# A two-segment hand-over in an attention plus gated feed-forward block: where the attention's buffers are closed, where a norm takes its rows from, and when weights and pieces are made

## The chip, the cores and the metric

One core of a Trainium2 chip runs the kernel. The metric is the device time of one execution in microseconds (us). The kernel before took 910.24 us (median of 3 runs, 908.57 to 913.8). All engines are named as in the profile: PE (TensorE matmul), PEld (its weight loads), DVE (VectorE), ACT (ScalarE), POOL (GpSimd), SP (SyncE, which issues nearly all DMAs).

## What is computed

The reference is a transformer block on x of 2048 x 512 in float32, with a modulation vector for each half:

```python
mod = (silu(c) @ w_mod).reshape(..., 6, 1, -1)          # sa, ca, ga, sb, cb, gb
h = layernorm(x) * (1 + ca) + sa
x = x + ga * attention(h)                               # "A"
h = layernorm(x) * (1 + cb) + sb
x = x + gb * ((h @ w_gate) * (h @ w_up)) @ w_down       # "B"
```

The attention has 32 heads of 16 and works in 4 segments of 512 rows. Within a segment it is a causal softmax, and its result is mixed with what a memory (M, z), summed over the earlier segments, answers to the queries. The output projection is `wo`. The second half is a bilinear feed-forward with 1376 hidden columns and no nonlinearity.

## The kernel before

**Number form.** Matmuls in float32 quality are made of three in a rounded format: each operand is split into a high part (an ACT copy that rounds) and a low part (a subtraction), and high x high, low x high and high x low are added up in PSUM. So every operand that PE reads costs one ACT copy and one subtraction on DVE or POOL. The weight halves are called cwH and cwL, those of the feed-forward's input bH and bL, those of the hidden values mH and mL, those of w_down dH and dL.

**Attention, lines 241 to 390 and 1061 to 1109.** The loop over `v` takes units of four heads (32 units, eight to a segment), each in five slots. A slot has matmuls of queries with keys for the row maximum (`q_step`, reduced on DVE), matmuls for the exponentials (`k_step`: one two-bank PSUM tile `lk`, one ACT `Exp` into `pt`, one or two triangular selects on POOL), and in slot 1 the product with the values (`av_step`, tile `tb`), then its transposition and division (`t_step`, tile `tr`, output `orow`). Other work is filled in between by the generators `fill_a` and `fill_b`: projections of the next segment, the memory, and, for finished segments, the output projection: `wo_op` transposes the attention's rows and splits them (op, oH, oL), `wo_mm` multiplies by `wo` (wops), `wo_add` (line 489) adds the result to the input rows `xr` and stores the sum to DRAM (`x1d`).

**Second norm, `lnC`, line 501.** It loads the four row tiles of a segment from `x1d`, takes mean and variance (DVE `cst`, `cmv`), the reciprocal root (ACT `csd` and `cy`, then five small POOL operations on `cya`, `cyb` and `cy`), normalises in place on DVE, transposes on PE (`ctp`, in the order 2, 3, 0, 1) and scales on ACT into `chf`. In the kernel before, segment 0 runs inside `fill_b`, segment 1 behind the attention's loop (line 1119) with tiles loaded back from `x1d`, segments 2 and 3 during the feed-forward (line 1387).

**Feed-forward, lines 1134 to 1417.** The 2048 rows are done as two halves `p` of two segments each. Each product with w_gate and w_up is a block product by Winograd's seven-multiplication scheme: `build(p)` makes seven pieces of the input out of `chf` (four differences `t` on POOL for two halves each, eight in all, then bH on ACT and bL on DVE), and `wprep` makes seven blocks out of two column tiles of weights: one load `cr` (512 KB), four small sums and differences `cs` on POOL, three ACT copies cwH and three POOL subtractions cwL. A `unit` (line 1284) is seven groups of six matmuls (line 1186) into PSUM tiles Z, Y and X, with ACT copies p5, p1, y and DVE additions c0, c1, c2 between them. Gate and up units alternate; POOL or DVE multiplies the two and `split` makes mH and mL. `wdprep` loads and scales w_down (`crd`) and makes dH and dL. `down` is six matmuls into a PSUM tile `acc` (line 1242) and a DVE addition to the row tile `xa` (line 1245). `prepare(n + 2)` runs in steps during unit n.

**Buffers.** Tiles come from pools with a number of buffers for each tag: `ap` (attention), `pw` (weights of the attention, then oH and oL), `wp` (wo raw, rows for wo_op), `bc` and `pb` (opened when the projections of the last segment are done), and `pc`, opened only when `ap`, `pw`, `wp` and `pb` are closed (lines 1128 to 1134), which holds all tiles of the feed-forward but chf and one of three weight sets.

**Order.** PE's order is written out by hand: every matmul depends on the one before it (`pe`, line 72), and DMAs and some DVE work are pinned to a place in it (`pin`). On the other engines a scheduler orders the instructions when the program is built, and each engine and the DMA queue of SP then run theirs strictly in that order. In the kernel before, the first weight set is prepared inside `fill_b` during the projection of segments 1 and 2; the pieces of the first half and the second weight set come behind the last `wo_add` (lines 1378 to 1381).

Of the kernel before, what the change touches and what calls it, by code (L numbers as in the profile page):

```python
# [57 lines left out]
def tile_kernel(ctx, tc, x, wq, wk_, wv, wo, beta, w_gate, w_up, w_down, c, w_mod, out):  # L58
# [306 lines left out]
    def t_step(u):  # L365

        s, g, jq = u // 8, u // 2 % 4, u % 2
        ug = u // 2
        h0 = jq * HQ
        if jq == 0:  # L370
            orows[ug] = ap.tile([P, 4, HG, DH], F32, tag="orow", name=f"orow{ug}", bufs=2)
# [29 lines left out]
    def wprep(n, tag, pool, rpool):  # L401

        nm, i = units[n % NU]
        raw = rpool.tile([P, KT, 2, P], F32, tag=f"raw{n % 2}", name=f"cr{n}", bufs=1)
        wh = pool.tile([P, 7, 2, P], F32R, tag=f"wh{tag}", name=f"cwH{n}", bufs=1)
        wl = pool.tile([P, 7, 2, P], F32R, tag=f"wl{tag}", name=f"cwL{n}", bufs=1)
        wslot[n] = wh, wl
        views = [w.rearrange("(k p) f -> p k f", p=P)[:, :, i * P:] for w in (w_gate, w_up)]
        gp = nc.gpsimd
        if nm == "x":  # L410
            m = ft[LAST][1]
            for j in range(2):
# [6 lines left out]
        pin(nc.sync.dma_start(raw.rearrange("p k r c -> p k (r c)"), views["gu".index(nm)][:, :, 0:2 * P]))  # L419
# [9 lines left out]
        gp.tensor_sub(S[:, 2], A(0, 0), A(1, 0))  # L429
        gp.tensor_sub(S[:, 3], A(0, 1), S[:, 1])  # L430
        yield
        top = raw[:, :, 0].rearrange("p (c k) f -> p c k f", c=2)
        for d, v in ((slice(4, 6), top), (6, A(1, 1)), (slice(0, 4), S)):
            act.activation(wh[:, d], v, AF.Copy)  # L434
            gp.tensor_sub(wl[:, d], v, wh[:, d].bitcast(F32))  # L435
            yield
# [34 lines left out]
    def xr_load(s, pool, tag="xr"):  # L471
        xrs = []
        for t in range(4):
            xr = pool.tile([P, D], F32, tag=tag, name=f"xr{s}_{t}", bufs=4)
            pin(nc.sync.dma_start(xr, x[rows(s, t), :]))
            xrs.append(xr)
        return xrs
# [20 lines left out]

    hfs = {}

    def lnC(s, pool, hpool, xpool, tag, nb, bk):

        xt = []
        for t in range(4):
            a = xpool.tile([P, D], F32, tag=tag, name=f"x1_{s}_{t}", bufs=nb)
            pin(nc.sync.dma_start(a, x1d[s][t]))
            xt.append(a)
        yield 0.1
# [376 lines left out]

    def open_b():
        close(papool)
        B["bcpool"], B["bc"] = open_pool(name="bc", bufs=1, side="right", reuse_waits="tile")
        B["pbpool"], B["pb"] = open_pool(name="pb", bufs=2, reuse_waits="tile")

    def wo_ops(s, rw, us):
# [77 lines left out]
    def fill_b():  # L969
# [3 lines left out]
            yield None  # L973
        us2 = []
        op2 = wo_op(2, B["o", 2], us2)
        xr1 = xr_load(1, pb)
        small = lambda name: bank(name, small=True)
# [134 lines left out]
    nq = [0]  # L1112

    def lqbank(name):
        nq[0] ^= 1
        return pst((P, 512), f"lq{nq[0]}", name)

    pb = B["pb"]
# [3 lines left out]
    btag[:] = ["sm"]  # L1122
    run(wo_op(3, o3, us3, (NG - 1,), True))
    run(lg)
    for t in range(4):
        run(wo_row(ps3[t], t, us3, (NG - 1,)))
        wo_add(3, t, xr3[t], ps3[t])
    close(B["pbpool"])
    close(pwpool)
    close(apool)  # L1130
    close(wppool)
    vec.eng = nc.vector

    pcpool, pc = open_pool(name="pc", bufs=2, reuse_waits="tile")
    bc = B["bc"]
    NT, NM = 13, 12

    def tmp(name):
        return pc.tile([P, L], F32, tag="t", name=name, bufs=NT)

    pieces = {}

    def build(p):

        def emit(j, srcs):
            hi = pc.tile([P, 2, L], F32R, tag=f"bh{j}", name=f"bH{p}_{j}", bufs=1)
            lo = pc.tile([P, 2, L], F32R, tag=f"bl{j}", name=f"bL{p}_{j}", bufs=1)
            for k in range(2):
                act.activation(hi[:, k], srcs[k], AF.Copy)
                vec.tensor_sub(lo[:, k], srcs[k], hi[:, k].bitcast(F32))  # L1150
# [54 lines left out]

    def split(p, f, c, h):
        n = ft[f][1]
        mH = pc.tile([P, L], F32R, tag="m", name=f"mH{p}_{f}_{c}", bufs=NM)
        mL = pc.tile([P, L], F32R, tag="m", name=f"mL{p}_{f}_{c}", bufs=NM)
        act.activation(mH[0:n], h[0:n], AF.Copy)  # L1210
        vec.tensor_sub(mL[0:n], h[0:n], mH[0:n].bitcast(F32))  # L1211
        mids[p, f, c] = mH, mL

    def wdprep(p, f):
        f0, n = ft[f]
        r = tmp(f"crd{p}_{f}")
        hi = pc.tile([P, D], F32R, tag="wdh", name=f"dH{p}_{f}", bufs=4)
        lo = pc.tile([P, D], F32R, tag="wdl", name=f"dL{p}_{f}", bufs=4)
# [6 lines left out]
        yield  # L1225

    def xtile(p, c, t):
        x1a[p, c, t] = pc.tile([P, D], F32, tag=f"xa{c}{t}", name=f"xa{p}_{c}_{t}", bufs=1)

    def xload2(p, c, t):  # L1230
        pin(nc.sync.dma_start(x1a[p, c, t], x1d[2 * p + c][t]))
# [27 lines left out]
    def finish(p, nm, f, c, v, psum):  # L1259

        n = ft[f][1]
        if nm == "g":
            if psum:
                r = tmp(f"gs{p}_{f}_{c}")
                act.activation(r[0:n], v[0:n], AF.Copy)
                v = r
            gs[p, f, c] = v
# [2 lines left out]
        (vec if psum else nc.gpsimd).tensor_mul(g[0:n], g[0:n], v[0:n])  # L1270
        split(p, f, c, g)

    def add(name, a, b, n=P):
        r = tmp(name)
        vec.tensor_add(r[0:n], a[0:n], b[0:n])  # L1275
        return r

# [85 lines left out]
    def prepare(n):  # L1363

        if n >= 2 * NU:
            return
        yield from wprep(n, n % 3, bc if n % 3 == 0 else pc, bc if n % 2 == 0 else pc)
        nm, i = units[n % NU]
        if nm == "u":
            yield from wdprep(n // NU, i)  # L1370
# [2 lines left out]
            yield from wdprep(n // NU, LAST)  # L1373

    half = [(c, t) for c in (1, 0) for t in range(4)]
    for c, t in half:
        xtile(0, c, t)
    pr1 = prepare(1)
    for _ in range(6):
        next(pr1)  # L1380
    run(build(0))
    DS = {"g": (1, 5, 6), "u": (1, 2, 4, 5, 6), "x": (1, 4, 6)}
    lgs = []

    def lns():
        for s in (2, 3):
            yield from lnC(s, pc, bc, pc, "t", NT, dbank)

    lg = lns()
    nb = None  # L1390
    for n in range(2 * NU):
        nm, i = units[n % NU]
        pr = prepare(n + 2)
# [5 lines left out]
        for st in (unit if nm != "x" else last_unit)(n):  # L1399
# [13 lines left out]
    d()  # L1413
    tail[1]()
    d(99)
    close(pcpool)
    close(B["bcpool"])


_INS = ["x", "wq", "wk", "wv", "wo", "beta", "w_gate", "w_up", "w_down", "c", "w_mod"]  # L1420
# [23 lines left out]
```

## Time and profile before

| | |
|---|---|
| median of 3 runs | 910.24 us |
| the profiled execution | 910.22 us, span of its instructions 908.5 us |
| instructions | 14393 |
| PE, DVE, POOL, ACT busy | 94%, 72%, 55%, 53% of the span |
| DMA | 105.70 MB, mean 116 GB/s |

Times in the profile count from the span's start. A row of the timeline has the start, the time from its first start to its last end, engine, line, operation, output<-inputs, and in brackets the idle time in front and what ended it. A row of the chain of work that ended last has start, time and what ran. A row of a table of windows has, for each engine, the busy time and the number of instructions, then the clock granted to TensorE as a share of full speed. Matmuls overlap in the pipeline, so one of 0.39 us stands for about 0.23 us of PE's time.

### The profile page before, as it was taken

What the parts mean: (1) busy time and instruction counts of PE and PEld (TensorE: products, weight loads), DVE (VectorE), ACT (ScalarE), POOL (GpSimd) and SP (SyncE); (2) the same over time, 40 slices, a digit from 0 to 9 for tenths busy, and PEclk for the clock granted to TensorE, in tenths of its full rate; (3) what the DMA queues carried; (4) which work ended last, traced back from release to release, by engine and by line L of the source; (5) the groups of instructions that cost most, each with busy time, mean ns of one, the idle gap of its engine ahead of it and who ended that gap; (6) DMA issues with size and microseconds to landing.
All of it is one profiled execution on the core that took longest, in us unless ns stands there. A gap on an engine that the chain in (4) does not pass through costs nothing.

```text
span 908.5 us, 14393 instructions
## 1 busy us (share of the span) xinstructions
PE 853.1 (94%) x4963; PEld 598.7 (66%) x4964; DVE 652.7 (72%) x1712; ACT 479.8 (53%) x732; POOL 502.7 (55%) x615
## 2 busy tenths in 40 slices
PE   8989999999999899999999876999999899999998
PEld 5756655556656565665656554778787777877776
DVE  8698777888788877888885463675849965646644
ACT  3658766787576865776445363343345534233320
POOL 4546535566464763955253169765658995566310
PEclk9999999999999999999999988999999999999999
DMA  7555435454454463564743352312221145111002
GB/s 232 154 149 152 125 99 158 128 158 128 117 158 117 135 169 100 146 194 163 227 153 125 125 209 69 87 56 70 70 61 33 46 127 170 56 46 37 12 1 92
DMA packets 77561, 105.70 MB, mean 116 GB/s; under 512 B 11760, under 2 KB 48624, under 8 KB 77488
## 3 DMA queue, kind: packets, MB, share of 16 engines
q1 hardware_dynamic: 77344, 104.76, 39.0%
q8 instruction: 39, 0.64, 0.3%
q14 instruction: 34, 0.28, 0.1%
q10 hardware_dynamic: 144, 0.02, 0.0%
HBM read 76.43 MB, written 28.05 MB: 115 GB/s over the span
## 4 chain that ended last, share of the span: by engine, by line
PE 68%; DVE 15%; ACT 7%; POOL 3%; DMA 3%; issue 3%; SPq 0%; DVEq 0%; ACTq 0%; POOLq 0%
PE acc L1242 11%; PE tb L85 7%; PE q L85 6%; PE k L85 6%; PE Xg L1186 5%; PE Xu L1186 5%; PE vps L85 5%; DVE q L39 4%; PE wops L85 4%; PE kps L85 3%; PE Yu L1186 3%; PE qps L85 3%; PE Yg L1186 2%; ACT pt L331 2%; PE Zu L1186 1%
## 5 line engine op out<-in xcount | busy, mean ns | idle before, releaser
L39 DVE CUSTOM_DVE_ANT_0 q<-q,cmask 128x384 f32<-128x384 f32 (+3 forms) x512 | 246.5, 508 | 49.5 <-PE q L85 39.3
L331 ACT ACTIVATE pt<-k 128x1024 f32<-128x1024 f32 x160 | 163.8, 1024 | 64.0 <-PE k L85 63.3
L337 POOL TENSOR_SCALAR_AFFINE_SELECT pt<-pt 128x256 f32<-128x256 f32 (+1 forms) x224 | 96.7, 446 | 172.0 <-ACT pt L331 169.6
L85 PE MATMUL q<-kst,qst 96*128 96x384 bf16 (+3 forms) x512 | 101.7, 300 | 10.9 <-DVE nm L39 9.8
L85 PE MATMUL k<-qst,kst 98*128 98x384 bf16 (+3 forms) x512 | 97.6, 303 | 7.1 <-ACT pt L331 7.0
L1245 DVE TENSOR_TENSOR xa<-xa,acc 128x512 f32<-128x512 f32 x95 | 64.8, 682 | 47.4 <-PE acc L1242 45.7
L85 PE MATMUL tb<-pt,v 128*32 128x512 f32 (+3 forms) x1024 | 75.5, 436 | 0.0
L85 PEld LDWEIGHTS <-kst 98*128 98x128 bf16 x512 | 38.0, 99 | 52.0 <-issue 45.8
L39 DVE DVE_READ_ACCUMULATOR2_ANT nm<- 128x1 f32 x512 | 72.0, 141 | 0.0
L1242 PE MATMUL acc<-dH,mL 128*128 128x512 f32 (+1 forms) x174 | 68.5, 394 | 1.3 <-DVE mL L1211 1.3
L1242 PE MATMUL acc<-dH,mH 128*128 128x512 f32 (+1 forms) x174 | 68.5, 394 | 0.0
L1242 PE MATMUL acc<-dL,mH 128*128 128x512 f32 (+1 forms) x174 | 68.2, 392 | 0.0
L85 PEld LDWEIGHTS <-qst 96*128 96x128 bf16 x512 | 43.2, 97 | 37.1 <-issue 13.3
L435 POOL TENSOR_TENSOR cwL<-cs,cwH 128x1024 fp32r<-128x1024 f32 x20 | 52.4, 2624 | 4.0 <-ACT cwH L434 4.0
L85 PEld LDWEIGHTS tb<-pt,v 128*32 128x32 f32 x1024 | 28.7, 109 | 38.6 <-issue 34.6
L435 POOL TENSOR_TENSOR cwL<-cr,cwH 128x512 fp32r<-128x512 f32 (+1 forms) x40 | 43.7, 1112 | 12.7 <-ACT cwH L434 12.7
L1270 POOL TENSOR_TENSOR c0g<-c0g,c0u 128x512 f32<-128x512 f32 x10 | 12.9, 1293 | 60.7 <-DVE c0u L1275 46.6
L1186 PE MATMUL Xu<-bH,cwH 128*128 128x512 f32 (+1 forms) x88 | 36.1, 410 | 6.2 <-DVE c2u L1275 4.0
L363 ACT ACTIVATE tsb<-tb 128x512 f32<-128x512 f32 x32 | 19.0, 594 | 40.2 <-PE tb L85 40.2
L1242 PEld LDWEIGHTS acc<-dH,mL 128*128 128x128 f32 (+1 forms) x174 | 32.8, 189 | 9.3 <-DVE mL L1211 2.3
L1242 PEld LDWEIGHTS acc<-dH,mH 128*128 128x128 f32 (+1 forms) x174 | 32.8, 189 | 8.2 <-ACT mH L1210 0.4
L1242 PEld LDWEIGHTS acc<-dL,mH 128*128 128x128 f32 (+1 forms) x174 | 32.7, 188 | 7.1
(278 smaller groups left out, 2177.4 us busy)
## 6 DMA issues: line engine op xcount, KB each, us to landing
wm<-in_w_mod_dram SPq DMA_DIRECT2D x24, 256.0 KB, 4.1
kd<-k SPq DMA_DIRECT2D x16, 384.0 KB, 2.5
kst<-kd SPq DMA_DIRECT2D x32, 192.0 KB, 3.2
qd<-q SPq DMA_DIRECT2D x16, 384.0 KB, 2.9
qst<-qd SPq DMA_DIRECT2D x32, 192.0 KB, 3.6
cr<-in_w_gate_dram SPq DMA_DIRECT2D x10, 512.0 KB, 4.1
cr<-in_w_up_dram SPq DMA_DIRECT2D x10, 512.0 KB, 3.9
crd<-in_w_down_dram SPq DMA_DIRECT2D x20, 256.0 KB, 2.7
```

The lines of the kernel that those rows point to most:

```text
L39: i = getattr(self.eng, name)(*a, **k)
L85: return pe(nc.tensor.matmul(*a, **k))
L331: ex = act.activation(pt, kp, AF.Exp, scale=0.25)
L337: sels[u, i] = nc.gpsimd.affine_select(w, w, pattern=[[0, w.shape[1]], [1, P]], compare_op=ALU.is_ge, fill=0.0, base=0, channel_multiplier=-1)
L363: act.activation(tsbs[u], tbs.pop(u), AF.Copy)
L435: gp.tensor_sub(wl[:, d], v, wh[:, d].bitcast(F32))
L1186: pe(nc.tensor.matmul(ps[0:n], a, b[:, k], start=first and c == 0, stop=last and c == 5, skip_group_check=True))
L1242: pe(nc.tensor.matmul(ps, a[0:m, t * P:(t + 1) * P], b[0:m], start=j == 0, stop=j == n - 1))
L1245: vec.tensor_add(xa, xa, ps)
L1270: (vec if psum else nc.gpsimd).tensor_mul(g[0:n], g[0:n], v[0:n])
```

## The change

The attention's pool is opened on the other side of the memory and closed as soon as the attention's loop ends, so that the feed-forward's pool (now in two parts, `pcA` there and `pcB` once `pb` is closed) opens before the last output projection. To that end the last `orow` comes from `pb`; the feed-forward's hidden values and w_down halves take over tags of `pw` in a fixed rotation (`KQ`, `WV`: six pairs for mH and mL, four for dH and dL, as many as before), its row tiles take tags of `wp` and `pw`, raw w_down takes two `wor` buffers, and `cs` has one buffer instead of two. The temporary tiles are 8 in `pcA` and 6 (gate values) in `pcB`, instead of 13.

`lnC` can take its tiles from outside: segment 1 uses the `xr` tiles that `wo_add` has just summed, without loading them back, and runs in `fill_b` during the projection of segment 2. Segment 0's norm moves one projection earlier, its loads ahead of those of `xr1`. The first weight set moves from the projection of segments 1 and 2 to that of segment 2.

The second weight set and the seven pieces are given out in steps beside the last projection's matmuls. The norms of segments 2 and 3 advance in two of three steps only.

```diff
-    apool, ap = open_pool(name="ap", bufs=1)
+    apool, ap = open_pool(name="ap", bufs=1, side="right")
...
-        S = rpool.tile([P, 4, 2, P], F32, tag=f"ws{n % 2}", name=f"cs{n}", bufs=1)
+        S = B["bc"].tile([P, 4, 2, P], F32, tag="ws", name=f"cs{n}", bufs=1)
...
-    def lnC(s, pool, hpool, xpool, tag, nb, bk):
+    def lnC(s, pool, hpool, xpool, tag, nb, bk, xt=None):
...
-        xr1 = xr_load(1, pb)
-        lg = lnC(0, pb, bc, pb, "x1", 7, small)
-        pr = (0.0 for _ in wprep(0, 0, bc, bc))
-        mm = weave(wo_mm(1, B["us1"], xr1), lg, (3, 6, 8, 10, 12, 14))
-        yield from weave(weave(mm, op2, (0, 5, 9, 13)), pr, (6,))
+        lg = lnC(0, pb, bc, pb, "xr", 12, small)
+        next(lg)
+        xr1 = xr_load(1, pb)
+        mm = weave(wo_mm(1, B["us1"], xr1), lg, (2, 3, 4, 5, 6, 7, 8, 9, 10, 11, 12, 13, 14))
+        yield from weave(mm, op2, (0, 5, 9, 13))
         yield from op2
+        yield from lg
         xr2 = xr_load(2, pb)
-        yield from weave(weave(wo_mm(2, us2, xr2), lg, (0, 2, 4, 6, 8, 10, 12, 14)), pr, (1, 4, 8, 10, 12))
+        lg = lnC(1, pb, bc, None, None, 0, small, xr1)
+        pr = (0.0 for _ in wprep(0, 0, bc, bc))
+        mm = weave(wo_mm(2, us2, xr2), lg, (0, 1, 2, 3, 4, 6, 7, 8, 9, 10, 11, 12, 13))
+        yield from weave(mm, pr, (0, 3, 5, 7, 9, 11, 13))
...
-    lg = lnC(1, pb, B["bc"], pb, "x1", 7, lqbank)
-    rows3 = (w for t in range(4) for w in wo_row(ps3[t], t, us3, range(NG - 1)))
-    run(weave(rows3, lg, (0, 0, 0, 0, 0, 0, 2, 3, 4, 5, 7, 8, 9, 10)))
...
-    close(B["pbpool"])
-    close(pwpool)
     close(apool)
-    close(wppool)
+    pcApool, pcA = open_pool(name="pca", bufs=1, side="right", reuse_waits="tile")
-    NT, NM = 13, 12
+    NT, NM = 8, 6
+    RING = {"wd": KQ[0:4], "m": KQ[4:8] + WV[0:2]}
+    def pair(kind, names):
+        tags = RING[kind][nring[kind] % len(RING[kind])]
+        nring[kind] += 1
+        return [pw.tile([P, 512], F32R, tag=tg, name=nm, bufs=1) for tg, nm in zip(tags, names)]
...
+    pr1 = prepare(1)
+    next(pr1)
+    nb = build(0)
+    next(nb)
+    rows3 = (w for t in range(4) for w in wo_row(ps3[t], t, us3, range(NG - 1)))
+    both = (0.0 for a in (pr1, nb, nb, pr1, nb, pr1, nb, pr1, nb, pr1, nb, pr1) if next(a, 0) is None)
+    run(weave(rows3, both, range(12)))
+    run(wo_op(3, o3, us3, (NG - 1,), True))
+    for t in range(4):
+        run(wo_row(ps3[t], t, us3, (NG - 1,)))
+        wo_add(3, t, xr3[t], ps3[t])
+    run(nb)
+    close(B["pbpool"])
+    pcBpool, pcB[0] = open_pool(name="pcb", bufs=1, reuse_waits="tile")
...
-            if 3 <= n < NU - 1:
+            nlg[0] += 3 <= n < NU - 1
+            if 3 <= n < NU - 1 and nlg[0] % 3:
                 next(lg, None)
```

More of the change, by code (lines that the diff above doesn't have):

```diff
@@ L370, in t_step @@
         if jq == 0:
-            orows[ug] = ap.tile([P, 4, HG, DH], F32, tag="orow", name=f"orow{ug}", bufs=2)
+            own = ug < NSEG * NG - 1
+            orows[ug] = (ap if own else B["pb"]).tile([P, 4, HG, DH], F32, tag="orow", name=f"orow{ug}", bufs=2 if own else 1)
             if s > 0:
@@ L473, in xr_load @@
         for t in range(4):
-            xr = pool.tile([P, D], F32, tag=tag, name=f"xr{s}_{t}", bufs=4)
+            xr = pool.tile([P, D], F32, tag=tag, name=f"xr{s}_{t}", bufs=4 if tag == "x" else 12)
             pin(nc.sync.dma_start(xr, x[rows(s, t), :]))
@@ L499, in tile_kernel @@
     hfs = {}
-    def lnC(s, pool, hpool, xpool, tag, nb, bk):
[L503 to L508, printed above, removed]
+    def lnC(s, pool, hpool, xpool, tag, nb, bk, xt=None):
+        if xt is None:
+            xt = []
+            for t in range(4):
+                a = xpool.tile([P, D], F32, tag=tag, name=f"x1_{s}_{t}", bufs=nb)
+                pin(nc.sync.dma_start(a, x1d[s][t]))
+                xt.append(a)
+            yield 0.1
         mv = pool.tile([P, 4, 2], F32, tag="mv", name=f"cmv{s}", bufs=2)
@@ L887, in open_b @@
         close(papool)
-        B["bcpool"], B["bc"] = open_pool(name="bc", bufs=1, side="right", reuse_waits="tile")
+        B["bcpool"], B["bc"] = open_pool(name="bc", bufs=1, reuse_waits="tile")
         B["pbpool"], B["pb"] = open_pool(name="pb", bufs=2, reuse_waits="tile")
@@ L975, in fill_b @@
         op2 = wo_op(2, B["o", 2], us2)
+        small = lambda name: bank(name, small=True)
+        lg = lnC(0, pb, bc, pb, "xr", 12, small)
+        next(lg)
         xr1 = xr_load(1, pb)
[L977 to L981 removed]
+        mm = weave(wo_mm(1, B["us1"], xr1), lg, (2, 3, 4, 5, 6, 7, 8, 9, 10, 11, 12, 13, 14))
+        yield from weave(mm, op2, (0, 5, 9, 13))
         yield from op2
+        yield from lg
         xr2 = xr_load(2, pb)
         B["orl_free"] = True
[L985 removed]
+        lg = lnC(1, pb, bc, None, None, 0, small, xr1)
+        pr = (0.0 for _ in wprep(0, 0, bc, bc))
+        mm = weave(wo_mm(2, us2, xr2), lg, (0, 1, 2, 3, 4, 6, 7, 8, 9, 10, 11, 12, 13))
+        yield from weave(mm, pr, (0, 3, 5, 7, 9, 11, 13))
         yield from lg
@@ L1111, in tile_kernel @@
     ps3 = [bank(f"wops3_{t}", shape=(P, 512)) for t in range(4)]
[L1112 to L1118, printed above, removed]
-    lg = lnC(1, pb, B["bc"], pb, "x1", 7, lqbank)
-    rows3 = (w for t in range(4) for w in wo_row(ps3[t], t, us3, range(NG - 1)))
-    run(weave(rows3, lg, (0, 0, 0, 0, 0, 0, 2, 3, 4, 5, 7, 8, 9, 10)))
[L1122 to L1127, printed above, removed]
-    close(B["pbpool"])
-    close(pwpool)
     close(apool)
-    close(wppool)
     vec.eng = nc.vector
-    pcpool, pc = open_pool(name="pc", bufs=2, reuse_waits="tile")
+    pcApool, pcA = open_pool(name="pca", bufs=1, side="right", reuse_waits="tile")
     bc = B["bc"]
-    NT, NM = 13, 12
+    pcB = [None]
+    NT, NM = 8, 6
+    KQ = [(f"w{a}H{i}", f"w{a}L{i}") for i in range(NG) for a in "kq"]
+    WV = [(f"wvH{i}", f"wvL{i}") for i in range(4)]
+    RING = {"wd": KQ[0:4], "m": KQ[4:8] + WV[0:2]}
+    XT = {(c, t): (wpool, "orl", 4) if c else (pw, WV[2 + t // 2][t % 2], 1) for c in range(2) for t in range(4)}
+    nring = {"wd": 0, "m": 0}
+    def pair(kind, names):
+        tags = RING[kind][nring[kind] % len(RING[kind])]
+        nring[kind] += 1
+        return [pw.tile([P, 512], F32R, tag=tg, name=nm, bufs=1) for tg, nm in zip(tags, names)]
     def tmp(name):
-        return pc.tile([P, L], F32, tag="t", name=name, bufs=NT)
+        return pcA.tile([P, L], F32, tag="t", name=name, bufs=NT)
     pieces = {}
@@ L1145, in emit @@
         def emit(j, srcs):
-            hi = pc.tile([P, 2, L], F32R, tag=f"bh{j}", name=f"bH{p}_{j}", bufs=1)
-            lo = pc.tile([P, 2, L], F32R, tag=f"bl{j}", name=f"bL{p}_{j}", bufs=1)
+            hi = pcA.tile([P, 2, L], F32R, tag=f"bh{j}", name=f"bH{p}_{j}", bufs=1)
+            lo = pcA.tile([P, 2, L], F32R, tag=f"bl{j}", name=f"bL{p}_{j}", bufs=1)
             for k in range(2):
@@ L1207, in split @@
         n = ft[f][1]
-        mH = pc.tile([P, L], F32R, tag="m", name=f"mH{p}_{f}_{c}", bufs=NM)
-        mL = pc.tile([P, L], F32R, tag="m", name=f"mL{p}_{f}_{c}", bufs=NM)
+        mH, mL = pair("m", (f"mH{p}_{f}_{c}", f"mL{p}_{f}_{c}"))
         act.activation(mH[0:n], h[0:n], AF.Copy)
@@ L1215, in wdprep @@
         f0, n = ft[f]
-        r = tmp(f"crd{p}_{f}")
-        hi = pc.tile([P, D], F32R, tag="wdh", name=f"dH{p}_{f}", bufs=4)
-        lo = pc.tile([P, D], F32R, tag="wdl", name=f"dL{p}_{f}", bufs=4)
+        r = wpool.tile([P, D], F32, tag="wor", name=f"crd{p}_{f}", bufs=2)
+        hi, lo = pair("wd", (f"dH{p}_{f}", f"dL{p}_{f}"))
         pin(nc.sync.dma_start(r[0:n], w_down[f0:f0 + n, :]))
@@ L1227, in xtile @@
     def xtile(p, c, t):
-        x1a[p, c, t] = pc.tile([P, D], F32, tag=f"xa{c}{t}", name=f"xa{p}_{c}_{t}", bufs=1)
+        pool, tg, nb = XT[c, t]
+        x1a[p, c, t] = pool.tile([P, D], F32, tag=tg, name=f"xa{p}_{c}_{t}", bufs=nb)
     def xload2(p, c, t):
@@ L1263, in finish @@
             if psum:
-                r = tmp(f"gs{p}_{f}_{c}")
+                r = gtile(f"gs{p}_{f}_{c}")
                 act.activation(r[0:n], v[0:n], AF.Copy)
@@ L1271, in finish, with gtile @@
         split(p, f, c, g)
+    def gtile(name):
+        return pcB[0].tile([P, L], F32, tag="g", name=name, bufs=NM)
     def add(name, a, b, n=P):
-        r = tmp(name)
+        r = (gtile if name[2] == "g" else tmp)(name)
         vec.tensor_add(r[0:n], a[0:n], b[0:n])
@@ L1366, in prepare @@
             return
-        yield from wprep(n, n % 3, bc if n % 3 == 0 else pc, bc if n % 2 == 0 else pc)
+        yield from wprep(n, n % 3, (bc, pcA, pcB[0])[n % 3], bc if n % 2 == 0 else pcA)
         nm, i = units[n % NU]
@@ L1375, in tile_kernel @@
     half = [(c, t) for c in (1, 0) for t in range(4)]
+    pr1 = prepare(1)
[5 more added lines that the diff above has]
+    run(weave(rows3, both, range(12)))
+    btag[:] = ["sm"]
+    run(wo_op(3, o3, us3, (NG - 1,), True))
+    for t in range(4):
+        run(wo_row(ps3[t], t, us3, (NG - 1,)))
[3 more added lines that the diff above has]
+    pcBpool, pcB[0] = open_pool(name="pcb", bufs=1, reuse_waits="tile")
     for c, t in half:
         xtile(0, c, t)
[L1378 to L1381, printed above, removed]
     DS = {"g": (1, 5, 6), "u": (1, 2, 4, 5, 6), "x": (1, 4, 6)}
@@ L1386, in lns @@
         for s in (2, 3):
-            yield from lnC(s, pc, bc, pc, "t", NT, dbank)
+            yield from lnC(s, pcB[0], bc, pcA, "t", NT, dbank)
     lg = lns()
-    nb = None
+    nlg = [0]
     for n in range(2 * NU):
@@ L1415, in tile_kernel @@
     d(99)
-    close(pcpool)
+    close(pcBpool)
     close(B["bcpool"])
+    close(pwpool)
+    close(pcApool)
+    close(wppool)
 _INS = ["x", "wq", "wk", "wv", "wo", "beta", "w_gate", "w_up", "w_down", "c", "w_mod"]
```

## The prediction, made before the changed kernel ran

> **What bounds the kernel now.** I read the page's span and 40 slices first, then windows of 100 us, then PE's waits between attention and feed-forward. A windows row has start and end, length, busy time (and instructions) of PE, PEld, DVE, ACT and POOL, then granted clock, DMA share, GB/s.
>
> ```profile
> span 908.5 us, 14393 instructions
> ```
> ```profile
> 506.90:577.80 70.90, 50.27 (x197) 36.48 (x195) 40.62 (x56) 29.70 (x53) 48.06 (x43) 0.90 0.40 136
> 518.50:523.80 5.30, 4.89 (x17) 3.53 (x18) 1.34 (x3) 1.56 (x2) 0.00 (x0) 0.68 0.00 0
> 590.00:690.00 100.00, 99.50 (x447) 79.03 (x446) 67.45 (x93) 40.99 (x71) 60.36 (x56) 1.00 0.21 60
> ```
>
> In the third row PE is busy throughout at full clock: what is saved on another engine there is worth nothing. The first row is the hand-over: it begins with the first transposition for the last output projection and ends with the first `acc`:
>
> ```profile
> 506.92 1.60 PE L88 MATMUL op<-ident,orl 128*128 128x128 f32 x12
> ```
> ```profile
> 577.85 0.99 PE acc L1242 x2
> ```
>
> Of its 70.9 us PE is busy 50.3, at a clock of 0.90; POOL is busy 48.1. What PE waits for between 505 and 580 (total, times, longest):
>
> ```profile
> PE Yu L1186 <- ACT cwH L434: 6.0, 1, 6.0
> PE ctp L88 <- DVE x L39: 3.2, 1, 3.2
> PE Yg L1186 <- ACT p5g L1295: 2.3, 1, 2.3
> PE Yg L1186 <- DVE bL L1150: 1.9, 1, 1.9
> PE Yu L1186 <- POOL cwL L435: 1.6, 1, 1.6
> PE acc L1242 <- DVE mL L1211: 1.3, 2, 1.1
> PE Zu L1186 <- POOL cwL L435: 1.3, 1, 1.3
> PE Zg L1186 <- DVE bL L1150: 0.9, 1, 0.9
> PE wops L85 <- ACT oH L460: 0.7, 1, 0.7
> PE tr L88 <- DVE oL L39: 0.4, 1, 0.4
> ```
>
> Nearly all of it is the lateness of weights, pieces and segment 1's norm, the three things that the change gives out sooner. From 580 on the order of PE's matmuls is the same in both kernels, but for a few transpositions. So the sum has three terms: the hand-over (A), what is pushed into the stretch ahead of it (B), and the buffer rotations behind it (C).
>
> **A, the hand-over.** PE's work, from the chain of waits:
>
> ```profile
> 502.77 2.29 PE tb L85 x32
> ...
> 505.95 0.44 PE ctp L88 x4
> ```
> ```profile
> 587.09 1.40 PE Yu L1186 x6
> ```
>
> Six matmuls take 1.40 (a group of three half of it), four transpositions 0.44. The stretch holds 26 sixes and 9 fours: 36.4 + 4.0 = 40.4. Segment 1's four `ctp` groups leave it (1.8): 38.6 remain. Weights and pieces now start beside the first `wops`, so the cwH, bL and ctp waits go. What is late next: the last unit's chain oH, oL, tr (0.7 + 0.4 above, plus about 0.2), one X group that waits for an ACT copy (estimate 1), and POOL, whose 48.1 us of work ahead of the first `acc` leave a part behind. Without segment 1's five small norm operations, two weight differences and one select that move out, some 39 us of POOL work stand between about 4 us after the first `op` and the last `c2g` product: it fits a stretch of 43, with about 2 us of PE waiting inside. I take 38.6 + 4.4 = **43**, a gain of 27.9. Bounds: 40.8 (only 2.2 of waits left), and 51, if POOL runs at its slow rows:
>
> ```profile
> 524.97 2.51 POOL L1157 TENSOR_TENSOR t<-chf,chf 128x512 f32<-128x512 f32 x2 [7.08 <-ACT chf L538]
> ...
> 540.85 1.73 POOL L1157 TENSOR_TENSOR t<-chf,t 128x512 f32<-128x512 f32 x1
> ```
>
> One `t` takes 1.25 with DVE idle and 1.73 beside DVE's `bL`. With all eight `t`, the products and the weight sums at the slow price, POOL needs 45.5 instead of 39, and PE's waits come later in its chain: 51. I choose 43, since in before the slow rows already stand in the 48.1.
>
> A rule of the Trainium skill speaks against this part: "SBUF — State Buffer", section "Who interferes with whom", has a DVE operation with two SBUF inputs and a GpSimd operation that reads SBUF exclude each other on a shared port, and the pieces now lie beside `oL` and `bL`, which are such operations. The trace agrees by the two rows above; by the rule the sum would be the slow one, which is the second rival.
>
> **B, ahead of the hand-over.** The first weight set moves out of the projection of segment 1, where its load blocked ACT and through it PE:
>
> ```profile
> 462.36 0.56 SPq L419 DMA_DIRECT2D cr<-in_w_gate_dram  x1
> ```
> ```profile
> 468.27 0.94 ACT L434 ACTIVATE cwH<-cr 128x512 fp32r<-128x512 f32 x2 [3.40 <-DMA cr<-in_w_gate_dram]
> ```
> ```profile
> 470.65 0.60 PE L85 MATMUL k<-qst,kst 98*128 98x384 bf16 x4 [2.07 <-ACT pt L331]
> ```
>
> That wait of 2.07 does not go: the same copy stands ahead of an `Exp` of the last unit now, and PE's k matmuls behind it. I put the two against each other, with ±2 for the range.
>
> New is segment 1's norm as a serial chain. The load is issued on SP behind the store of segment 1's last sum and the last `xr2` load:
>
> ```profile
> 484.24 0.69 DVE L39 TENSOR_TENSOR xr<-xr,wops 128x512 f32<-128x512 f32 x1 [0.56 <-PE wops L85]
> 485.53 0.21 DVE L39 COPY nt<-ntp 32x128 bf16<-32x128 bf16 x1 [0.60 <-PE ntp L88]
> 485.67 0.52 DVE L39 TENSOR_SCALAR x<-x,cmv,cy 128x512 f32<-128x512 f32 x1
> ```
> ```profile
> 487.01 0.52 SPq L475 DMA_DIRECT2D xr<-in_x_dram  x1
> ```
>
> That sum (0.69) comes right after `nt` and ends at about 486.5; store and `xr2` load take SP some 0.8, so the weight load is issued at about 487.3. In before it took 5.9 (462.36 to 468.27, the release of ACT): 493.2. POOL's order in after puts between this load and segment 1's `cy` the whole weight set:
>
> ```profile
> 469.01 0.72 POOL L429 TENSOR_TENSOR cs<-cr 128x256 f32<-128x256 f32 x1
> 469.69 1.26 POOL L435 TENSOR_TENSOR cwL<-cr,cwH 128x512 fp32r<-128x512 f32 x1
> ...
> 471.59 0.73 POOL L435 TENSOR_TENSOR cwL<-cr,cwH 128x256 fp32r<-128x256 f32 x1
> ...
> 474.56 2.37 POOL L435 TENSOR_TENSOR cwL<-cs,cwH 128x1024 fp32r<-128x1024 f32 x1 [0.45 <-ACT cwH L434]
> ...
> 500.02 0.77 POOL L337 TENSOR_SCALAR_AFFINE_SELECT pt<-pt 128x256 f32<-128x256 f32 x2 [1.16 <-ACT pt L331]
> ```
> ```profile
> 517.13 0.20 POOL L524 TENSOR_TENSOR cyb<-cyb,cya 128x4 f32<-128x4 f32 x1
> ```
>
> Four sums 2.9, three differences 1.26 + 0.73 + 2.37 = 4.4, four selects 1.5, five small operations 1.4 with their gaps: 10.2, so `cy` at 503.4. Then DVE: four normalisations (2.1), one addition that stands among them (0.69) and a division (about 0.7): 506.8. PE stands ready for the first `ctp` at about 500 and waits 6 to 7 us, because that group is now ahead of the last unit's product with the values (`tb`). Behind it come 4 ctp groups (1.76), four threes (2.8) and `tb` with its last three (2.3 + 0.7): 7.6. A wait this long costs clock too; the row for 518.50 to 523.80 follows a ctp wait of 3.2 and has 5.3 us at 0.68: 1.7 lost. So the first `op` comes at 506.8 + 7.6 + 1.7 = **516.1**, 9.2 later than 506.92. Bounds: 0 (the load lands at once and POOL's order has slack) and 12 (slow POOL rows).
>
> By the Trainium skill, "TensorE: Matmul & The Clock Gate", section "Part 1: The HAM clock gate", the clock falls to half after an idle window of about 3.4 us and comes back after as much work: for this wait the same 1.7. But here the clock fell after the shorter 3.2 as well, so I'd not lean on that threshold for waits of 2 to 3 us.
>
> **C, behind it.** mH and mL used to take any free one of twelve buffers; now six pairs rotate. In five places (once in the first half, four times in the second) the pair asked for is still read by the `acc` of two column tiles before, and ACT's mH and DVE's mL come only after it:
>
> ```profile
> 577.12 0.68 DVE L1211 TENSOR_TENSOR mL<-c2g,mH 128x512 fp32r<-128x512 f32 x1
> ```
>
> DVE's row is 0.68, an ACT copy of this size 0.47 (0.94 for the two cwH above): 1.2, and with two hand-overs between engines up to 1.5 a place, against a cover of one six (1.40). So 0 to 7.5 in all; I take **1.7**, near the lower end, because in all places but the last that six lies between. Eight temporaries and six gate tiles instead of thirteen, one `cs`, two raw w_down: I cost them at nothing, since DVE, ACT and POOL have 30 to 60% idle behind 590 and wait there anyway; what happens without that cover is the last rival. Norms of segments 2 and 3 at two thirds of the pace are hidden by the same stretch. Four loads less on SP change nothing, as SP sets no end here.
>
> **Sum**: 910.2 − 27.9 + 9.2 + 1.7 = **893**. The profiled execution stands at the median (910.22 and 910.24), so no correction.
>
> **Rivals.** (1) B is hidden or short: the load lands by 491, C is nothing, the hand-over takes 40.8; op at 512. 910.2 + 5 − 30.1 = 885. For it: PE has matmuls to lend ahead of `tb`; against: they are in a fixed order. (2) POOL becomes the bound of the hand-over, by the slow rows: 51 instead of 43, 901. For it: 48.06 of 70.90 busy already, and eight `t` beside DVE work. (3) The change doesn't do what it says: pieces and weights can be asked for early but are not made early, because the new pool's tiles lie in the attention's memory and the last unit's readers, or the loads, are late; the gain shrinks to the ctp part (3.2 + 1.8 and the clock, some 12): 910.2 − 12 + 9.2 + 1 = 908. (4) Slower: in units 3 to 10 the rows of segments 2 and 3 hold four of the eight temporaries, and a unit has p5, p1, y and three sums to place in the other four. If a sum waits for POOL's product (1.73 for one of this size beside DVE) PE waits for the PSUM tile behind it: 3 us and 1.6 of clock in each of 8 to 9 units, 33 to 40 us, for 926 to 933. From 2.1 us per unit, clock included, the gain is gone. Against: in the third window above POOL is only 60% busy, so its products come soon after their sums.
>
> **How the numbers follow.** Chances: forecast 0.50 (own range 888 to 898: A ±3, B ±2, C 0 to 4), first rival 0.13, second 0.17, third 0.08, fourth 0.12. The range 882 to 908 holds the first three and half of the third rival, 0.84. What can be told from no change is 0.5%, 4.6 us: under 905.7 is faster, which takes forecast and rivals one and two: 0.80; the third is the same, 0.08; the fourth slower, 0.12.
>
> **What would show it.** In the profile of after: a wait of `ctp` for DVE `xr` of 5 to 7 us near 500; the first `op` near 516; no wait of 6.0 for cwH and none for bL between `op` and `acc`; the first `acc` near 559; k's wait of 2 us near 494 instead of 470.65; at most five short waits of `acc` for mH or mL; a span of about 891. The forecast is wrong if `op` comes near 507 (B not paid), if the stretch from `op` to `acc` is over 48 (POOL bound), or if PE is less than 95% busy between 600 and 690 (the fourth rival).

## The result: slower by 0.9%

The changed kernel took 917.89 us (median of 7 runs, 915.87 to 920.95) against 910.24 before: ratio 1.0089, 95% interval 1.0063 to 1.0114. The forecast was 893, with a range of 882 to 908. It missed the size and the sign.

Page of after, the span, the engines, and PE's busy tenths and clock in 40 slices:

```profile
span 914.7 us, 14403 instructions
...
PE 855.6 (94%) x4963; PEld 599.0 (65%) x4964; DVE 664.7 (73%) x1712; ACT 478.4 (52%) x732; POOL 508.8 (56%) x615
...
PE   8989999999999899999988769999999889999998
...
PEclk9999999999999999999999879999999999999999
```

The dip of PE's busy tenths is still there, in slices 21 to 24 (457 to 549 us), down to 6 as before. Only 6.2 us of span separate the kernels, and these are the difference of larger parts. To find them I cut both traces at the same matmuls: ntp of unit 29 and of unit 31 (the transposition of a unit's row maxima), the first `op` of segment 3, the first Zg, the first Zu, the first `acc`. Worked out from the starts of these rows in one profiled execution of each, in us:

| stretch | before | after | difference |
|---|---|---|---|
| start to ntp 29 | 455.6 | 456.2 | +0.6 |
| ntp 29 to ntp 31 (segment 0's norm now here) | 29.6 | 33.6 | +4.0 |
| ntp 31 to first op | 21.7 | 31.4 | +9.7 |
| first op to first Zg | 23.5 | 28.3 | +4.8 |
| first Zg to first Zu | 14.5 | 8.3 | −6.2 |
| first Zu to first acc | 30.2 | 18.5 | −11.7 |
| first acc to the end | 333.4 | 338.5 | +5.1 |

The first `acc` matmul of before starts at 575.08. The chain row at 577.85, which the prediction took for it, is a later one: before's hand-over was 68.2 us long and not 70.9. After's is 55.1 (521.14 to 576.19).

So 18 us are gained between Zg and acc, where weights and pieces were late, and 24 us are lost around it. Windows of after, in the columns of the prediction's, for op to Zg, Zg to acc, and 100 us behind it:

```profile
521.14:549.47 28.33, 17.68 (x70) 13.80 (x69) 26.04 (x25) 11.79 (x21) 21.98 (x15) 0.76 0.21 69
549.47:576.20 26.73, 25.67 (x110) 20.06 (x108) 16.78 (x17) 12.09 (x22) 20.01 (x16) 1.00 0.51 172
576.20:680.00 103.80, 102.11 (x442) 81.08 (x441) 69.77 (x100) 39.10 (x68) 67.12 (x64) 0.98 0.23 73
```

From Zg to acc PE is now busy 25.67 of 26.73 at full clock: next to nothing is left to gain there. Ahead of Zg it is busy 17.68 of 28.33 at a clock of 0.76, and DVE 26.04 of 28.33: DVE has become the busiest engine. PE's waits from 505 to 600, after:

```profile
PE wops L85 <- DVE oL L465: 6.8, 1, 6.8
PE ctp L88 <- DVE xr L39: 2.9, 3, 2.1
PE wops L85 <- ACT oH L461: 2.0, 1, 2.0
PE acc L1238 <- DVE mL L1207: 1.7, 2, 1.4
PE tr L88 <- DVE oL L39: 1.6, 1, 1.6
```

The waits for cwH (6.0) and bL (1.9) are gone, as forecast. In their place stands one wait of 6.8 for the last group's `oL`, and 2.0 for its `oH`. DVE and POOL there, and PE behind them, by the timeline of after:

```profile
526.10 9.16 DVE L1147 TENSOR_TENSOR bL<-chf,bH 128x512 fp32r<-128x512 f32 x6
535.18 1.21 DVE L1216 TENSOR_TENSOR crd<-crd,gbb 128x512 f32<-128x512 f32 x1
536.31 6.23 DVE L1147 TENSOR_TENSOR bL<-t,bH 128x512 fp32r<-128x512 f32 x4
542.47 1.74 DVE L1218 TENSOR_TENSOR dL<-crd,dH 128x512 fp32r<-128x512 f32 x1
544.13 0.68 DVE L465 TENSOR_TENSOR oL<-op,oH 128x512 fp32r<-128x512 f32 x1
```
```profile
527.87 3.43 POOL L1154 TENSOR_TENSOR t<-chf,chf 128x512 f32<-128x512 f32 x2
531.27 3.44 POOL L1154 TENSOR_TENSOR t<-chf,t 128x512 f32<-128x512 f32 x2
```
```profile
544.86 0.80 PE L85 MATMUL wops<-woH,oL 128*128 128x512 f32 x1 [6.78 <-DVE oL L465]
```

`oL` is ready to run when ACT's oH is (537.5), but DVE's order has ten bL, a crd and a dL ahead of it. Each of the first six bL takes 1.53 us on the mean. In before six of them took 3.69, 0.61 each, because POOL stood idle:

```profile
531.20 3.69 DVE L1150 TENSOR_TENSOR bL<-chf,bH 128x512 fp32r<-128x512 f32 x6
```

So the pieces moved to a place where the two engines slow each other, and the attention's last step was queued behind them.

Ahead of the hand-over, after's PE, POOL, DVE and SP:

```profile
481.89 0.63 PE L88 MATMUL ctp<-ident,x 128*128 128x128 f32 x4 [2.43 <-DVE oL L39]
...
507.69 0.33 PE L88 MATMUL ctp<-ident,xr 128*128 128x128 f32 x1 [2.10 <-DVE xr L39]
...
511.45 4.09 PE L85 MATMUL tb<-pt,v 128*32 128x512 f32 x32
```
```profile
503.88 2.37 POOL L436 TENSOR_TENSOR cwL<-cs,cwH 128x1024 fp32r<-128x1024 f32 x1
506.21 0.20 POOL L528 TENSOR_TENSOR cy<-cy,cyb 128x4 f32<-128x4 f32 x1
```
```profile
506.44 0.60 DVE L39 TENSOR_SCALAR xr<-xr,cmv,cy 128x512 f32<-128x512 f32 x1 [9.37 <-POOL cy L528]
```
```profile
492.59 0.45 SPq L420 DMA_DIRECT2D cr<-in_w_gate_dram  x1
```

Two things are seen. Segment 0's transpositions share a PSUM tile with the `op` of segment 2, so the first row's ctp waits until DVE has read that `op`. And segment 1's cy does come behind the whole weight set: DVE idles 9.37 us for it, PE waits, and then `tb` runs at little more than half pace (4.09 us instead of 2.29, at a granted clock of 0.57).

### The profile page after: what moved, and what is told of

Same layout as the page of the kernel before. It is cut to its first block, busy times and chain, and to the rows that moved or that the text cites. A ratio compares the mean times of both kernels' runs of the same rounds, so it can differ in the third digit from the quotient of the medians.

```text
span 914.7 us, 14403 instructions
## 1 busy us (share of the span) xinstructions
PE 855.6 (94%) x4963; PEld 599.0 (65%) x4964; DVE 664.7 (73%) x1712; ACT 478.4 (52%) x732; POOL 508.8 (56%) x615
## 4 chain that ended last, share of the span: by engine, by line
PE 68%; DVE 17%; ACT 6%; issue 3%; POOL 2%; DMA 2%; SPq 1%; ACTq 0%; DVEq 0%; POOLq 0%
PE acc L1238 12%; PE tb L85 7%; PE Xg L1183 6%; PE q L85 6%; PE Xu L1183 6%; DVE q L39 5%; PE k L85 5%; PE vps L85 4%; PE Yg L1183 3%; PE Yu L1183 3%; PE kps L85 3%; PE wops L85 3%; PE qps L85 2%; DVE bL L1147 2%; ACT pt L331 2%
## 5 line engine op out<-in xcount | busy, mean ns | idle before, releaser
L436 POOL TENSOR_TENSOR cwL<-cs,cwH 128x1024 fp32r<-128x1024 f32 x20 | 53.5, 2676 | 10.2 <-ACT cwH L435 10.1
L436 POOL TENSOR_TENSOR cwL<-cr,cwH 128x512 fp32r<-128x512 f32 (+1 forms) x40 | 46.3, 1173 | 14.1 <-ACT cwH L435 14.1
L1238 PEld LDWEIGHTS acc<-dH,mL 128*128 128x128 f32 (+1 forms) x176 | 33.2, 189 | 15.7 <-DVE mL L1207 8.1
L1238 PEld LDWEIGHTS acc<-dL,mH 128*128 128x128 f32 (+1 forms) x176 | 33.2, 189 | 7.2
```

Source lines behind the costliest of these rows:

```text
L1238: pe(nc.tensor.matmul(ps, a[0:m, t * P:(t + 1) * P], b[0:m], start=j == 0, stop=j == n - 1))
```

## The experiments

Two theories stood at the start. **Queues**: the loss comes from where single instructions stand in strict orders, cy behind cwL, oL behind bL, acc behind the ring's old reader. **Rival**: DVE's and POOL's work on the pieces is what bounds the hand-over, wherever single instructions stand. All against the kernel before on the same chip, whose own median there was 909.6 to 911.6, so that the ratios compare better than the times. The edits below are shortened and stand against the changed kernel.

| run | us | ratio, 95% interval |
|---|---|---|
| changed kernel | 917.9 | 1.0089 (1.0063 to 1.0114) |
| e1_oL_ahead | 917.4 | 1.0063 (1.0040 to 1.0086) |
| e2_t_on_dve | 919.2 | 1.0089 (1.0056 to 1.0122) |
| e3_two_rings | 915.0 | 1.0040 (1.0020 to 1.0060) |
| e4_weights_early | 918.7 | 1.0075 (1.0051 to 1.0098) |
| e6_norms_as_before | 909.7 | 0.9993 (0.9983 to 1.0004) |
| e7_norms_oL_rings | 905.9 | 0.9940 (0.9915 to 0.9964) |
| e8_also_t_on_dve | 906.6 | 0.9949 (0.9931 to 0.9967) |
| e9_pieces_ahead_of_op | 896.2 | 0.9852 (0.9835 to 0.9869) |
| e10_oL_then_pieces | 894.0 | 0.9827 (0.9801 to 0.9852) |

And the stretches of these runs in us, from the same matmuls as above, of one profiled execution each:

| run | ntp 29 to ntp 31 | to first op | op to Zg | Zg to Zu | Zu to acc | acc to end |
|---|---|---|---|---|---|---|
| after | 33.6 | 31.4 | 28.3 | 8.3 | 18.5 | 338.5 |
| e1 | 35.3 | 31.6 | 15.5 | 19.1 | 18.4 | 339.7 |
| e2 | 36.8 | 31.1 | 32.0 | 8.8 | 18.0 | 333.4 |
| e3 | 35.2 | 31.5 | 28.4 | 8.2 | 18.5 | 333.8 |
| e4 | 42.3 | 24.2 | 28.6 | 7.9 | 18.7 | 339.5 |
| e6 | 29.8 | 28.6 | 30.6 | 7.0 | 18.0 | 336.3 |
| e7 | 28.7 | 29.0 | 17.6 | 20.5 | 18.7 | 332.3 |
| e8 | 30.7 | 28.6 | 19.7 | 20.0 | 18.7 | 332.8 |
| e9 | 28.1 | 25.2 | 22.1 | 11.1 | 18.3 | 331.2 |
| e10 | 28.6 | 25.2 | 19.4 | 9.1 | 18.9 | 332.0 |

**e1_oL_ahead.**

```diff
+    for _ in range(5): next(rows3)
+    run(wo_op(3, o3, us3, (NG - 1,), True))     # was behind rows3
...
+    tc.add_manual_dep(bL.ins, last_oL.ins.name, NOSYNC)   # in emit(): each bL behind that oL on DVE
```

> The last unit's transposition for the output projection comes after five groups of wops instead of after twelve, and every bL of the first build is ordered behind its oL on DVE. The queue theory (oL stands on DVE behind ten bL of 1.5 us, PE waits 6.8 us for it and then runs slow) says: no PE wait for oL of over 1 us, first Zg at about 539 instead of 549.5, first acc 6 to 11 us earlier, time about 907 to 912 against 917.9 of the changed kernel. The rival (the pieces themselves, with POOL and DVE taking turns, set the end) says: Zg is earlier, but the same time is then waited for bL or cwL before the first acc, and the time stays at 916 to 918.

The wait for oL went and Zg came 13 us sooner after op (15.5 instead of 28.3). But Zu came only 2 us sooner: 11 of the 13 were waited for again, at the next group. e1's waits from 505 to 600, and DVE there:

```profile
PE Yg L1185 <- DVE xr L492: 9.5, 1, 9.5
```
```profile
543.09 3.41 DVE L1148 TENSOR_TENSOR bL<-t,bH 128x512 fp32r<-128x512 f32 x2
546.43 1.21 DVE L1220 TENSOR_TENSOR dL<-crd,dH 128x512 fp32r<-128x512 f32 x1
547.56 0.68 DVE L492 TENSOR_TENSOR xr<-xr,wops 128x512 f32<-128x512 f32 x1
548.16 0.68 DVE L1148 TENSOR_TENSOR bL<-t,bH 128x512 fp32r<-128x512 f32 x1
548.76 1.27 DVE L492 TENSOR_TENSOR xr<-xr,wops 128x512 f32<-128x512 f32 x2
```

Yg needs the PSUM tile of a `wops`, and the addition that reads it stands behind the bL, two of which (543.09) take 1.7 us each. The time is the rival's: 917.4 is the same as 917.9 within both intervals. But this wait, too, is one for a short operation behind bL, and the edit also lets the pieces start later (the first bL 9.4 us behind op, in after 5.0). So e1 does not separate the two theories; the additions to xr ahead of the bL were not tried.

**e2_t_on_dve.**

```diff
-                nc.gpsimd.tensor_sub(t, a[k], b[k])
+                (nc.gpsimd if p else vec).tensor_sub(t, a[k], b[k])
```

> The eight differences t of the first build run on DVE instead of POOL; nothing else changes. If DVE and POOL shut each other out (bL 1.53 us beside t, 0.61 alone), DVE's bL fall to about 0.65 and DVE has done ten bL and eight t in about 13 us where ten bL took 15.4: the wait for oL falls from 6.8 to 2 to 4 us, POOL makes the second weight set 8 us sooner, time 911 to 914. If it is only the number of operations ahead of oL on DVE (eight more), the wait for oL grows by some 5 us, time 921 to 924.

The wait for oL rose from 6.8 to 10.1: the number of operations ahead of it won. With POOL idle behind them the last six bL took 4.14, 0.69 each, but those beside POOL's weight set 1.15. So both halves of the expectation are partly true, the time, 919.2, lies in neither range, and neither theory is settled by it. From the first acc on this run is 5 us shorter than after. The two traces show where: 2.7 up to the next Zu (clock 1.00 instead of 0.79, waits for mL of 0.85 instead of 1.69), 1.4 in a later unit (from 711 in after, from 714 in e2; clock 1.00 instead of 0.91, the same waits), and 0.9 by a shorter wait for mL (2.01 instead of 2.91).

**e3_two_rings.**

```diff
-    RING = {"wd": KQ[0:4], "m": KQ[4:8] + WV[0:2]}
+    RING = {"wd": KQ[0:4], "m0": KQ[4:7], "m1": KQ[7:8] + WV[0:2]}
...
-        mH, mL = pair("m", ...)
+        mH, mL = pair(f"m{c}", ...)
```

> The six pairs for mH and mL rotate as two rings of three, one for each half's segment c, instead of one ring of six. If the rotation causes the waits of acc for mL (6.0 us in five places, against 1.3 before) and the loss of 6 us after 680, those waits fall to below 2 us and the time to 912 to 914. If the loss there has another cause (POOL's and DVE's load in the second build, the smaller number of temporaries), the waits and the time stay, 916 to 919.

PE's waits from the first acc to the end, after and then e3:

```profile
PE acc L1238 <- DVE mL L1207: 6.0, 5, 2.9
PE Xu L1183 <- DVE c1u L1274: 5.4, 4, 3.1
```
```profile
PE Xu L1183 <- DVE c1u L1274: 5.2, 4, 3.1
PE acc L1238 <- DVE mL L1207: 1.7, 2, 1.4
```

The waits fell as expected; the time, 915.0, by a little less. The 1.7 that stay are the two waits at the first acc, which before has too (1.3); so the rotation's own were three, of 2.91, 0.88 and 0.48. The units in which they lie get 2.6, 1.2 and 1.0 us shorter. From acc to the end e3 takes 333.8, before 333.4, and all five runs with two rings take 331.2 to 333.8, the other five 333.4 to 339.7. So the rotation explains 4.7 of the 5.1 lost there, and the smaller number of temporaries costs nothing that shows.

**e4_weights_early.** The first weight set's generator goes back into the projections of segments 1 and 2.

```diff
-        pr = (0.0 for _ in wprep(0, 0, bc, bc))   # with segment 2's projection
+        pr = (0.0 for _ in wprep(0, 0, bc, bc))   # from step 6 of segment 1's on
```

> The first weight set is prepared where the kernel before has it, during the projections of segments 1 and 2; all else as in the changed kernel. If POOL's weight set ahead of cy delays segment 1's norm, cy is done 5 to 7 us sooner (about 500 instead of 506.4), the ctp wait of 2.9 goes, the first op comes at 514 to 517 instead of 521.1, but k waits about 2 us for the Exp near 470 again; time 913 to 917. If the transpositions of segment 0's norm ahead of it are what costs, op stays at 520 or later and the time at 917 to 919.

Both outcomes at once. From ntp 31 to op it takes 24.2 instead of 31.4: the weight set ahead of cy cost 7 us, as the first half says. But from ntp 29 to 31 it takes 42.3 instead of 33.6. There the weight set now meets segment 0's norm, so that op comes at 522.4 after all. DVE idles for cy, and PE for the q reductions queued behind that:

```profile
472.29 0.75 DVE L39 TENSOR_SCALAR x<-x,cmv,cy 128x512 f32<-128x512 f32 x1 [5.32 <-POOL cy L528]
```
```profile
474.02 0.58 PE L85 MATMUL q<-kst,qst 96*128 96x512 bf16 x1 [2.86 <-DVE nm L39]
```

**e6_norms_as_before.** Segment 0's norm and the weight set as in the kernel before; segment 1's norm from `xr1`, its transpositions behind `tb`.

```diff
+        mm = weave(wo_mm(1, ...), lg, (3, 6, 8, 10, 12, 14)); yield from weave(weave(mm, op2, ...), pr, (6,))
...
+        mm = weave(weave(wo_mm(2, ...), lg, (0, 2, 4, 6, 8, 10, 12, 14)), pr, (1, 4, 8, 10, 12))
+        yield from weave(mm, lg1, (3, 5, 7, 9, 10, 11, 12, 13, 14))
```

> Segment 0's norm and the first weight set stand where the kernel before has them; segment 1's norm keeps the projection's own tiles, but its statistics and transpositions come behind segment 0's, behind the last tb. Rings, pools and pieces as in the changed kernel. If the loss ahead of the hand-over (op 14 us later) comes from where these two norms and the weight set stand in the strict orders of PE, DVE and POOL, the first op comes at 507 to 511 and the stretch from op to the first acc stays at 53 to 56: time 904 to 908. If the loss comes from segment 1's norm being there at all, op stays at 516 or later and the time at 913 to 918.

The time is 8 us less than after and the same as the kernel before; it lies between the two ranges, with op at 516.1. ntp 29 to 31 is back at 29.8, and op comes 58.4 behind ntp 29 instead of 65.0 (before 51.3). The place of the norms and weights was worth 6.5 of the 13.7 us; of the rest 3.7 are waits of segment 1's ctp (2.8) and the first op (0.9) for ACT's chf, one after another on a single PSUM tile, and 1.8 the four ctp groups themselves, which before has behind op. Another 2.2 of the 8 us are gained at the first acc, where the clock was 1.00 and not 0.79.

**e7_norms_oL_rings** and **e8_also_t_on_dve.** e6 with the edits of e1 and e3; then also that of e2.

> The three edits together: norms and first weight set as in the run before this one, the last oL ahead of the bL, two rings for mH and mL. If the three causes are separate and add up (about 10 ahead of op, 3.5 up to the third unit, 4.5 behind it), the time is 897 to 902, below the kernel before. If a gain in one place is only waited for in the next, it stays at 904 to 910.

> As e7_norms_oL_rings, with the eight differences t of the first build on DVE. With oL ahead of them they hold up no wops any more, so only the taking of turns between DVE and POOL decides: if it sets the end of the pieces (PE waits 9.5 us for bL in e1_oL_ahead), that wait falls by 3 to 6 us and the time to 893 to 898. If the number of DVE operations decides (22 instead of 14), it is 898 to 906.

e7 gains on both kernels, but less than the sum: as in e1, 13 us are saved ahead of Zg and lost ahead of Zu. What it gains on e6 is the 4.0 behind acc, the rings. e8, just above both its ranges, is no better. Both wait nearly as long for the same thing, here e7 and then e8:

```profile
PE Yg L1185 <- DVE xr L492: 10.3, 1, 10.3
```
```profile
PE Yg L1185 <- DVE xr L492: 9.8, 1, 9.8
```

What is left to try is the start of the pieces. POOL and DVE of e7 ahead of the first `t` and the first bL:

```profile
520.50 1.65 POOL L388 TENSOR_TENSOR orow<-orow,memb 128x512 f32<-128x512 f32 x1 [17.69 <-DVE orow L39]
```
```profile
526.66 0.69 DVE L465 TENSOR_TENSOR oL<-op,oH 128x512 fp32r<-128x512 f32 x1 [5.64 <-ACT oH L461]
527.27 2.28 DVE L1148 TENSOR_TENSOR bL<-chf,bH 128x512 fp32r<-128x512 f32 x2
```

POOL idles 17.69 us and DVE 5.64, with segment 0's rows long there.

**e9_pieces_ahead_of_op.** The pools are open by then, so the pieces of segment 0 need not wait for `op`.

```diff
+    nb = build(0); run(lg1)                     # ctp of segment 1 on two PSUM tiles in turn
+    for _ in range(3): next(nb)
     run(wo_op(3, o3, us3, range(NG - 1), True)) # was inside the last unit
+    # bH, bL of pieces 6, 7, 4 behind the last oH, oL
```

> As e7_norms_oL_rings, with the pieces of the first half given out ahead of the last output projection's transpositions: segment 1's ctp use two PSUM tiles in turn, the transpositions op come behind the first pieces, and oH and oL of the last group stand ahead of bH and bL of the last three pieces. If the pieces (14 bL and 8 t on DVE and POOL in turn, with the additions to xr queued behind them) bound the hand-over from the first op on, then starting them some 8 to 10 us sooner brings the second unit (Zu) from 551 to 541 to 546 and the time to 896 to 901. If something else holds that second unit (the weights' load, PE's order, PSUM), Zu stays at 550 to 552 and the time at 904 to 908.

As expected: 896.2. Zu comes 86.5 us behind ntp 29, in e7 95.8. DVE and PE of e9:

```profile
511.14 7.02 DVE L1150 TENSOR_TENSOR bL<-chf,bH 128x512 fp32r<-128x512 f32 x6 [2.42 <-ACT bH L1149]
518.09 1.88 DVE L466 TENSOR_TENSOR oL<-op,oH 128x512 fp32r<-128x512 f32 x3
```
```profile
519.42 0.80 PE L85 MATMUL wops<-woH,oH 128*128 128x512 f32 x1 [7.67 <-DVE oL L466]
```

The first bL begins 16 us sooner than in e7. But the run changes more than that: of the 9.3 us up to Zu 4.4 lie ahead of op, where the second PSUM tile takes the waits for chf from 3.7 to 0.4, and 4.9 behind it, and the parts were not tried one by one. Now the first three oL stand behind six bL, and PE waits 7.67.

**e10_oL_then_pieces.** Only the first piece ahead of these oL.

```diff
+    next(nb) x2 moved behind run(wo_op(3, ...)); bH, bL of all pieces but the first behind the oH, oL given out last
```

> As e9_pieces_ahead_of_op, but only the first piece goes ahead of the oH and oL of the first three groups; the others come behind them. In e9 PE waits 7.7 us for the first of these oL, behind six bL. If that wait was in series with the pieces, it falls to about 1 us and the time to 889 to 893. If the pieces, made by DVE and POOL in turn, bound the stretch in either order, the same time is waited for a few groups later (wops for the last oL, Yg for the addition to xr or for bL) and the time stays at 894 to 898.

The wait fell to 3.7 and Zu came 4.7 us sooner behind op (28.5 instead of 33.2). The time, 894.0, lies between what the two theories gave, and the intervals of e9 and e10 overlap, so how much of the 7.7 us was in series with the pieces stays open. It is the lowest of all: 1.7% under the kernel before.

## Why the prediction was wrong

**What bounds it** in before was read rightly: the waits for weights, bL and segment 1's norm inside the hand-over went, and from Zg to acc PE has only 1.1 us without work.

**A, the hand-over** (43 forecast, 55.1 measured). The step that failed is "what is late next". I listed oH, oL, tr at 1.3, from before's waits, where oL had an idle DVE; they measured 10.4 (2.0, 6.8 and 1.6), and from op to Zg the clock was 0.76, for which this part had no term. I asked which waits go, and did not ask what stands ahead of oL in DVE's order once bL begin sooner: ten bL. I also priced the meeting of the engines on POOL alone (t at 1.73 instead of 1.25), and gave DVE's bL no price; ten of them took 1.5 instead of 0.6 each. With the oL ahead of the bL (e1) the stretch up to Zu is only 2 us shorter; with the pieces begun sooner and a second PSUM tile besides (e9 against e7) the way from ntp 29 to Zu is 9.3 shorter. How much of the 12 us is the order on DVE and how much its work stays open. And since before's stretch was 68.2 and not 70.9, the same 43 would have been a gain of 25.2.

The second rival, POOL at its slow price, came nearest in its mechanism: the rule of the Trainium skill ("SBUF — State Buffer", "Who interferes with whom") that I weighed and set aside holds in this trace, where a bL (0.61 alone) and a t (1.25 alone) beside each other take some 1.5 to 1.7. But PE waited for DVE and not for POOL, and 901 was still too low. I was also wrong to count oL among the operations with two SBUF inputs: it reads op, which lies in PSUM, and it took 0.68 beside POOL's t. It was late by its place and not by its length.

**B, ahead of it** (+9.2 forecast for op; measured +14.2). The chain load, weight set, cy, normalisation, ctp was right in its order: POOL's part took 9.6 us from landing to cy (10.2 forecast), DVE's 3.3 (3.4), the load 4.2 (5.9); from the last normalisation to op it took 11.4 instead of 9.3, with 1.0 of waits for ACT's chf and the slow `tb`. But it began later, because SP issued the load at 492.59 instead of 487.3, behind `nt`. That was late because of what I had put at nothing: segment 0's ctp among the `op` of segment 2, on one PSUM tile, 2.43 and 0.87 and 0.70 us of PE's waiting, with 1.63 of wops for oL. The wait of k for the Exp that I set against it did go, and came back near 499 with 0.3 and not with the 2 that I said. With both moved back (e6) op comes 6.5 us sooner behind ntp 29.

**C, behind it** (+1.7 forecast; measured +5.1). The mechanism is right, e3 removes 4.7 of it; it showed in three places and not five. The term that was mis-sized is mL: I took 0.68 from one row of before, where others took up to 2.88. The longest of the three is this, DVE and POOL of after:

```profile
731.82 2.82 DVE L1207 TENSOR_TENSOR mL<-c2g,mH 128x512 fp32r<-128x512 f32 x1
```
```profile
731.25 2.84 POOL L436 TENSOR_TENSOR cwL<-cs,cwH 128x1024 fp32r<-128x1024 f32 x1
```

mL takes 2.82, and ends 0.55 after POOL's operation does, which is about its own length alone. The cover of one six (1.40) is then too short by far, and PE waits 2.91.

**The sum** by its terms: −13.1 (not −27.9), +13.7 ahead of op from ntp 29 (not +9.2), +5.1 (not +1.7), and 0.6 that was there before the change begins: +6.3, as the spans show (+6.2). The fourth rival (too few temporaries) did not happen: PE is busy 89.65 of the 90 us from 600 to 690. Its price was also added up wrongly: 4.6 us in 8 to 9 units are 37 to 41, not 33 to 40.

## What to carry to other kernels

When work is given out sooner, list for every engine what now stands behind it: the price of this change was not in the moved work but in the short operations that PE needed next (oL, cy, the addition that frees a PSUM tile). Removing one such wait only uncovered the next (13 us gained and 11 given back in e1). What moved the end was e9, which starts the pieces where the engines were idle and takes the transpositions off a single PSUM tile; which of the two did more is not shown. Price an operation by a row in which its neighbour engine is as busy as it will be.

## What the runs showed that was not expected

A DVE subtraction of 128x512 with both inputs in SBUF took 0.61 with POOL idle, 1.53 beside POOL's t, 1.15 beside its small sums cs, and 2.82 beside a cwL of 2.84. With one input in PSUM nothing of this shows: in after all 16 oL and all 96 additions to xa took 0.64 to 0.69, whatever POOL did.

The same instructions with the same waits took 33.6 us in after and 36.8 in e2 between ntp 29 and ntp 31, where the granted clock was 1.00 and 0.91:

```profile
456.17:489.79 33.62, 27.65 (x202) 17.11 (x200) 25.40 (x88) 16.04 (x21) 8.22 (x20) 1.00 0.34 107
```
```profile
455.82:492.60 36.78, 30.80 (x203) 18.09 (x201) 25.41 (x88) 16.04 (x21) 8.23 (x20) 0.91 0.30 93
```

PE's longest wait in both is 2.4 us. By the Trainium skill ("TensorE: Matmul & The Clock Gate", "Part 1: The HAM clock gate") the clock falls after an idle window of about 3.4 us; the second row has no such wait and a lower clock all the same. So a wait of about 2.4 us may cost 3 us of clock or nothing from one kernel to the next, and a difference of 3 us between two single profiles ahead of the hand-over proves nothing by itself.
